# Attention and expert mixture on one core: corrected costs in a hand-written issue order, and a second home for late output tiles

## The chip, the cores and the metric

One of the eight cores of a Trainium2 chip runs the whole kernel. The core has a matmul engine (TensorE, PE in the profile, with its weight loads as PEld), VectorE (DVE), ScalarE (ACT), GpSimd (POOL) and SyncE (SP), each with an instruction queue of its own that it works off in order. The metric is the device time of one execution in microseconds (us); lower is better.

## The reference

Sliding-window attention with four sink tokens, then a mixture of four experts that every token passes through, weighted by its normalised domain probabilities. B, H, S, D are 4, 8, 768, 64; the mixture has N = 3072 tokens, width 512, inner width 1024.

```python
scores = q @ k.T / sqrt(D)
keep = (key < 4) | ((query - key >= 0) & (query - key < 128))
a = softmax(where(keep, scores, -1e9))
x = (a @ v) as [B * S, H * D]
p = domain_probs / (domain_probs.sum(-1) + 1e-9)
out = sum over e of  p[:, e] * (relu(x @ w1[e]) @ w2[e])
```

## The kernel before

Everything is computed in bf16 with float32 sums in PSUM. Tokens are worked on in groups of 256 (a pair of 128-token blocks): three groups g for each of four batches b. Attention for batch b goes by head pairs: scores (L676), exponentials on ScalarE (L701), a mask on VectorE (L695, L710), values (L735 for the sinks, L742 for the window), a reciprocal of the row sums (L769) and a scaling by it. For batch 0 the scaling is one VectorE instruction (L772) and the result is turned by PE (L800). For the other batches the scaling is four ScalarE instructions of 64 columns for each head pair (L781), and once all four head pairs of a group are scaled, one transposing DMA on SP's queue turns the group into `xT` (L759). The rows of q and k of these batches are turned by transposing DMAs too (L241).

The mixture's first layer comes in two forms. A slow unit (b, g, e) is four steps of eight matmuls of 256 columns (L1050) with a relu on ScalarE or VectorE. A fast unit is a Strassen-like form with seven products P1 to P7 of sixteen matmuls of 128 columns each (L1137). Its results are passed on through ScalarE copies (L1183, L1196) and VectorE additions (L1190, L1205), and gated results (L1170) go into the tile `H`. It needs sums and differences of the turned tokens (`T`, L1106) and of the weights. The second layer of batch 0 is plain: eight matmuls of 512 columns (L1382) for each 128 tokens and expert, gathered by VectorE (L1394). The second layer of batches 1 to 3 is again a seven-product form over pairs (b, g): P1, P2, P6, P5, P7, P3, P4, each of four pieces, one for each expert (L1311), with differences of `H` made on VectorE ("chores", L1234 and L1255). Two PSUM banks `acc` alternate. The results are copied or added into one output tile `osb` (L1354, L1339, L1342, L1347) and stored from it on SP's queue (L1344, L1303).

There is no scheduler at run time. The order of all instructions is written out by a planner in Python while the kernel is built. It keeps a clock `t` for each engine and prices what it has ordered: `pe`, `act`, `dve`, `pool`, `lands` for the loads on POOL's queue, `sp` for those on SP's. Work that follows a matmul waits in a list `pend` with a ready time and a slack, and `flush` gives it to ScalarE or VectorE by its due time. The loop at L1440 looks at each step that could come next on PE (a step of attention, of the first layer, a product piece, a second-layer step of batch 0), takes one that is planned to be ready within 40 ns, and among these the one of the lowest priority number:

```python
opts.append((max(p, now), HIGH_PRODUCT if behind > BEHIND or mix.live >= FULL else LOW_PRODUCT, "product", None))
opts += [(max(f, now), p, "first", x) for f, p, x in mix.firsts()]
```

A first-layer step of the open unit number i (0 or 1) has the priority 2 + `STEP0` x i, a new unit beside an open one `OPEN` = 2.6. A step of attention has 1.5 when it is due. If nothing is ready within 220 ns and the planned time is below 20 us, the planner orders one idle matmul (`idle_products`, L549) on a block of zeros.

The planned times matter only through the order: on the chip each instruction waits for its semaphores, and what stands behind it on its engine waits with it.

Of the kernel before, what the change touches and what calls it, by code (L numbers as in the profile page):

```python
# [11 lines left out]
FP32 = mybir.dt.float32  # L12
BF16 = mybir.dt.bfloat16
# [3 lines left out]
def kernel(  # L17
# [12 lines left out]
    nc = tc.nc  # L30

    B, H, S, D = q.shape
# [3 lines left out]
    Ntok, Dout = out.shape  # L36

    P = 128
# [13 lines left out]
    G = 2 * P  # L52
# [10 lines left out]
    SHARE_OF = (0.98, 0.90, 1.01)  # L63
    LEAD = (0.91, 0.90)
    DUE = 1.5
    LOW_PRODUCT = 2.015
    LOW_SECOND = 2.7
    HIGH_PRODUCT = 1.9
    EARLY = 0.01
    MASK = 2500  # L70
    GATE = 800
    GATE0 = 500
    FORM = 9000
    TOKEN = 1000
    MARGIN = 2000
    HOLD = 0
    FULL = 7
    STEP0 = 0.01
    READY = 40
    WIDE = 2  # L80
    OPEN = 2.6
# [1 line left out]
    ONE = 2  # L83
    PAIR = 1
    BEHIND = 1500
    CHORES = 6
    OWN = 2
    BIASED = 1
    FAST = tuple(START)
# [7 lines left out]
    t = {"pe": 1200.0, "act": 0.0, "dve": 0.0, "pool": 1280.0, "sp": 800.0, "sw": 6500.0, "hw": 0.0}  # L97
    ring, whole = [0.0] * 6, [False] * 6
    WARM = 6600.0
    FLIP, LATE = 300, 2500  # L100

    def pe(cols, *deps, n=1, switch=0):
        t["pe"] = max([t["pe"], *deps])
# [3 lines left out]

    def act(cols, *deps):
        at = max([t["act"], *deps])
        t["act"] = at + 75 + cols / 1.2  # L110
        return at + 205 + cols / 1.2

    def dve(cols, *deps, rate=0.96, fixed=157):
        at = max([t["dve"], *deps])
# [376 lines left out]
    load_v(0, (2, 3))  # L491
    load_w1(0, 2, [0])
    load_w1(0, 2, [1])
    t["sw"] += 700
    load_w2(0)

    nc.vector.tensor_copy(out=ident, in_=identf)
# [221 lines left out]
    def values(b, hp, g):  # L719

        ready = values_ready(b, hp, g)
        slot = pick()
        od = bank(slot, [P, 2, 2, DX], FP32, "od")
        a = aTs.pop((b, hp, g))
        cols = 0
        for qi in range(2):
            qb = 2 * g + qi
            terms = []
            c = 0
            for (kb, q0, nq) in GROUPS[g]:  # L730
                if q0 <= qb < q0 + nq:
                    terms.append((kb, c + (qb - q0) * P))
                c += nq * P
            if g > 0:
                nc.tensor.matmul(  # L735
                    od[:, qi], lhsT=sinkA[b][:, (qb - 2) * P:(qb - 1) * P], rhs=vsd[b][:, hp],
                    start=True, stop=False, skip_group_check=True,
                )
                cols += 2 * DX
            for ph in range(2):  # L740
                for i, (kb, c) in enumerate(terms):
                    nc.tensor.matmul(  # L742
                        od[:, qi, ph], lhsT=a[:, ph, c:c + P], rhs=vx[kb][:, 2 * hp + ph, 0:DX],
                        start=(g == 0 and i == 0), stop=(i == len(terms) - 1), skip_group_check=True,
                    )
                    cols += DX + 5
        done = pe(cols, ready)
        ring[slot] = 1e12
        if (b, g) not in onats:
            onats[b, g] = sb.tile([P, 2, NHP, P], BF16, name="onat", tag="onat", bufs=2)  # L750
        o = onats[b, g]

        def scaled(at):
            take(slot, at)
            onat_at[b, hp, g] = at
            onat_n[b, g] = onat_n.get((b, g), 0) + 1
            if b and onat_n[b, g] == NHP:
                xT[b, g] = sb.tile([P, 2, NHP, P], BF16, name="xT", tag="xT", bufs=2 * NG)
                nc.sync.dma_start(  # L759
                    out=xT[b, g].rearrange("c q h p -> c (q h) p"),  # L760
                    in_=o.rearrange("p q h c -> p (q h c)"), transpose=True,
                )
                turned_out = sp(at, issue=1330, takes=1400, turning=True)
                for x in range(NHP):
                    xT_at[b, x, g] = turned_out

        def run(engine):
            R = sb.tile([P, 2, 2, 1], FP32, name="R", tag="R", bufs=6)
            nc.vector.reciprocal(out=R, in_=od[:, :, :, D:DX])  # L769
            at = dve(4, fixed=171)  # L770
            if b < ONACT:
                nc.vector.tensor_mul(  # L772
                    o[:, :, hp].rearrange("p q (h d) -> p q h d", h=2), od[:, :, :, 0:D], R.to_broadcast([P, 2, 2, D]),
                )
                scaled(dve(2 * P))
                return

            def multiply(engine):
                for qi in range(2):
                    for ph in range(2):  # L780
                        nc.scalar.mul(o[:, qi, hp, ph * D:(ph + 1) * D], od[:, qi, ph, 0:D], R[:, qi, ph])  # L781
                        at = act(D)
                scaled(at)
            later("act", at, 600, multiply)
        later("dve", done, 500, run)
        values_at[b, g] = done
# [130 lines left out]
    class Mixture:  # L917


        def __init__(self):  # L920
            self.early = {g: list(range(E)) for g in range(NG)}
            self.open = []
            self.units = []
            for b, g in PAIRS:
                fast = [e for e in range(E) if self.is_fast(b, g, e)]
                slow = [e for e in range(E) if e not in fast]
                while fast or slow:
                    for x in (fast, slow):
                        if x:
                            self.units.append((b, g, x.pop(0)))  # L930
            self.order = list(self.units)
            self.T, self.T_at, self.fast, self.finished = {}, {}, {}, set()
            self.second, self.live, self.since, self.turn, self.credit = [], 0, 0, 0, 0.0
            self.H, self.H_at, self.H_part = {}, {}, {}
            self.S, self.S_at, self.waiting, self.last = {}, {}, [], []
            self.products = [(b, g, m) for b, g in PAIRS for m in CHAIN]
            self.piece, self.chores = 0, 0
            self.at, self.S4_at, self.C22 = {}, {}, {}
            self.done = 0.0
            self.stored = []  # L940
            self.spare, self.lent = [], {}

        def is_fast(self, b, g, e):
# [330 lines left out]
        def product_ready(self):  # L1274
            if not self.products:
                return 1e12
            b, g, m = self.products[0]
            e = self.order_of(b, g)[self.piece]
            at = (self.H_at if m in ("P1", "P2") else self.S4_at if m == "P3" else self.S_at).get((b, g, e), 1e12)
            bank = self.bank(b, g, m)  # L1280
            if self.piece == 0:
                at = max(at, acc_free[bank])
            if m == "P1" and self.piece == E - 1 and acc_free[1 - bank] > 1e11:
                at = 1e12
            if self.second or self.open and not self.open[0]["unit"][0] or any(self.early.values()):
                return 1e12
            return max(at, forms_at.get((e, m), 0.0 if m in ("P1", "P2", "P3") else 1e12))

# [6 lines left out]
        def emit_product(self):  # L1295
# [4 lines left out]
            r = (b * NQB + 2 * g) * P  # L1300

            def store(at, c=slice(0, Dout)):
                nc.sync.dma_start(out=out[r + P:r + 2 * P, c], in_=out_sb[b, g][:, 1, c])  # L1303
                sp(at)
            bank = self.bank(b, g, m)
            other = acc[1 - bank][:, 0:G]
# [16 lines left out]
                return  # L1323
            self.products.pop(0)
            if m == "P1":
                out_sb[b, g] = mo.tile([P, 2, Dout], FP32, name="osb", tag="osb", bufs=1)
                self.C22[b, g] = join(2, lambda at: store(at))
            o = out_sb[b, g]
            C11, C12, C21, C22 = o[:, 0, 0:G], o[:, 0, G:], o[:, 1, 0:G], o[:, 1, G:]
            acc_free[bank], seeded = 1e12, acc_free[1 - bank]  # L1330
            if m == "P1" and not final:
                acc_free[1 - bank] = 1e12
# [1 line left out]
            def run(engine):  # L1334
                if m == "P1" and not final:
                    nc.scalar.copy(out=other, in_=x)
                    acc_free[0] = acc_free[1] = act(G, seeded)
                elif m == "P2" and final:
                    nc.vector.tensor_add(C11, C11, x)  # L1339
                    acc_free[bank] = dve(G)  # L1340
                elif m == "P3":
                    nc.vector.tensor_add(C12, C12, x)  # L1342
                    acc_free[bank] = at = dve(G)
                    nc.sync.dma_start(out=out[r:r + P, :], in_=o[:, 0])  # L1344
                    sp(at)
                elif m == "P7":
                    nc.vector.tensor_add(C22, C22, x)  # L1347
                    acc_free[bank] = at = dve(G)
                    if final:
                        store(at, slice(G, Dout))  # L1350
                    else:
                        self.C22[b, g](at)
                else:
                    nc.scalar.copy(out={"P1": C11, "P2": C11, "P6": C12, "P5": C22, "P4": C21}[m], in_=x)  # L1354
                    acc_free[bank] = at = act(G)
                    if m == "P4" and final:
                        store(at, slice(0, G))
                    elif m == "P4":
                        self.C22[b, g](at)
# [189 lines left out]
```

## Time and profile before

| | |
|---|---|
| time, median of 3 runs | 368.44 us (367.04 to 370.63) |
| time of the profiled execution | 369.98 us |
| its span, first to last instruction | 368.1 us |
| mean granted clock of PE | 0.995 |
| PE busy | 356.0 us, 97% of the span |
| VectorE busy | 298.9 us, 81% |
| ScalarE busy | 162.5 us, 44% |
| POOL busy | 71.2 us, 19% |
| DMA | 37.25 MB in 117291 packets, 101 GB/s |

The page slices the span into 40 parts of 9.2 us and gives the busy share of each engine in tenths. A row of a timeline or of the waits names the engine, the line of the kernel, the tiles written and read, and in brackets how long the engine stood idle before and what ended the idle time. A wait of an engine costs time only if that engine's work, or what depends on it, sets the end.

### The profile page before, as it was taken

Reading aid. Unit: us, or ns where it says so; the run is one execution under the profiler, and the core shown is the slowest. Engines: PE = TensorE matmul, PEld = TensorE weight load, DVE = VectorE, ACT = ScalarE, POOL = GpSimd, SP = SyncE. Lnnn points to the kernel's source line nnn. Section 1 sums busy time; section 2 is a strip of 40 time slices with the busy share of each in tenths; the row PEclk is TensorE's granted clock in tenths of the full one; section 3 lists DMA queues with packets and bytes.
Section 4 is the critical chain, followed back from the end, with each engine's and each line's share of the span. In section 5 each row is a group of like instructions: output and inputs, shape, how many; then the busy total and the mean of one; then the engine's idle time right before and its main releaser. Section 6 shows DMA issues by size and latency. Waiting matters only on the chain.

```text
span 368.1 us, 10528 instructions
## 1 busy us (share of the span) xinstructions
PE 356.0 (97%) x4395; PEld 298.2 (81%) x4407; DVE 298.9 (81%) x671; ACT 162.5 (44%) x415; POOL 71.2 (19%) x92
## 2 busy tenths in 40 slices
PE   8789999999989999999999999999999999999996
PEld 4466666766668768898899899899999999999985
DVE  6743898976779869969879988979999898898930
ACT  5824643477636643555464545555113312213110
POOL 8926117403500805001430000000000000000000
PEclk9989999999999999999999999999999999999999
DMA  9999999999985999917999210212012011010011
GB/s 165 170 184 199 210 207 146 145 177 101 172 93 117 131 193 171 82 61 87 131 172 144 55 63 23 51 57 72 20 35 76 23 52 52 30 59 2 3 59 57
DMA packets 117291, 37.25 MB, mean 101 GB/s; under 512 B 100612, under 2 KB 112740, under 8 KB 117244
## 3 DMA queue, kind: packets, MB, share of 16 engines
q0 software_dynamic: 77520, 17.31, 53.0%
q1 hardware_dynamic: 38668, 18.75, 25.3%
q8 instruction: 34, 0.56, 0.6%
q10 hardware_dynamic: 1056, 0.52, 0.5%
q14 instruction: 13, 0.11, 0.1%
HBM read 40.45 MB, written 6.34 MB: 127 GB/s over the span
## 4 chain that ended last, share of the span: by engine, by line
PE 84%; DMA 6%; DVE 4%; ACT 3%; issue 1%; POOL 1%; ACTq 0%
PE cps L1137 29%; PE acc L1311 29%; PE hps L1050 11%; PE acc L1382 8%; DMA w<-in_moe_w_dram 2%; PE sps L676 2%; PE od L742 2%; ACT onat L781 2%; DMA xT<-onat 2%; DMA vx<-in_v_dram 1%; DMA out_dram<-osb 1%; PE od L735 1%; DVE H L1170 1%; PE tx L800 0%; ACT aT L701 0%
## 5 line engine op out<-in xcount | busy, mean ns | idle before, releaser
L1137 PEld LDWEIGHTS <-w 128*128 128x128 bf16 x1152 | 71.2, 98 | 3.8 <-issue 1.5
L1311 PEld LDWEIGHTS <-H 128*128 128x128 bf16 x600 | 55.9, 98 | 6.6 <-issue 0.9
L1050 PE MATMUL hps<-xT,w 128*128 128x256 bf16 x384 | 49.7, 278 | 3.7 <-DMA w<-in_moe_w_dram 2.8
L1170 DVE SCALAR_TENSOR_TENSOR H<-cps,gates 128x512 bf16<-128x512 f32 x78 | 52.5, 683 | 0.9
L701 ACT ACTIVATE aT<-sps 128x512 bf16<-128x512 f32 (+1 forms) x96 | 47.4, 582 | 13.1 <-PE sps L676 13.0
L1137 PEld LDWEIGHTS <-vf 128*128 128x128 bf16 x744 | 45.6, 98 | 2.1 <-issue 1.1
L1311 PE MATMUL acc<-w,H 128*128 128x256 bf16 x360 | 47.2, 273 | 0.0
L781 ACT ACTIVATE onat<-od,R 128x64 bf16<-128x64 f32 x144 | 33.0, 321 | 31.8 <-DVE R L769 26.5
L1050 PEld LDWEIGHTS <-w 128*128 128x128 bf16 x384 | 36.7, 100 | 10.5 <-DMA w<-in_moe_w_dram 3.0
L1382 PE MATMUL acc<-w,H 128*128 128x512 bf16 x180 | 43.8, 379 | 0.7 <-issue 0.2
L1137 PE MATMUL cps<-T,w 128*128 128x128 bf16 x576 | 43.9, 219 | 0.3 <-DVE cps L1190 0.3
L1137 PE MATMUL cps<-xT,w 128*128 128x128 bf16 x576 | 43.6, 219 | 0.2 <-ACT onat L781 0.2
L1183 ACT COPY cps<-cps 128x512 f32<-128x512 f32 x36 | 20.8, 576 | 44.8 <-PE cps L1137 43.3
L1354 ACT COPY osb<-acc 128x256 f32<-128x256 f32 x36 | 13.6, 378 | 57.6 <-PE acc L1311 54.1
L1137 PE MATMUL cps<-T,vf 128*128 128x128 bf16 x496 | 36.5, 219 | 0.1
L294 POOL DMA_DIRECT2D vx<-in_v_dram x24 | 21.6, 908 | 65.2 <-PE od L742 52.7
L1382 PEld LDWEIGHTS <-H 128*128 128x128 bf16 x192 | 18.0, 98 | 17.5 <-issue 0.2
L1311 PEld LDWEIGHTS <-S 128*128 128x128 bf16 x288 | 27.0, 98 | 4.3 <-issue 1.5
L1190 DVE TENSOR_TENSOR cps<-H,cps 128x512 f32<-128x512 f32 x30 | 20.7, 691 | 7.6 <-PE cps L1137 5.4
L1063 ACT ACTIVATE H<-hps 128x512 bf16<-128x512 f32 x26 | 15.5, 598 | 23.3 <-PE hps L1050 23.2
L1205 DVE TENSOR_TENSOR H<-H,cps 128x512 f32<-128x512 f32 x30 | 20.5, 683 | 5.3 <-PE cps L1137 5.2
L695 DVE TENSOR_TENSOR aT<-aT,mask 128x1024 bf16<-128x1024 bf16 (+1 forms) x36 | 22.7, 639 | 2.4 <-ACT aT L701 2.3
(125 smaller groups left out, 555.6 us busy)
## 6 DMA issues: line engine op xcount, KB each, us to landing
w<-in_moe_w_dram POOLq DMA_DIRECT2D x7, 1024.0 KB, 16.5
out_dram<-osb SPq DMA_DIRECT2D x23, 256.0 KB
gates<-gate_rows SPq DMA_DIRECT2D x36, 128.0 KB
vx<-in_v_dram POOLq DMA_DIRECT2D x24, 128.0 KB, 8.0
qkn<-in_q_dram POOLq DMA_DIRECT2D x22, 128.0 KB, 8.2
qkn<-in_k_dram POOLq DMA_DIRECT2D x22, 128.0 KB, 8.2
w<-in_moe_w_dram POOLq DMA_DIRECT2D x2, 512.0 KB, 9.6
kraw<-in_k_dram ACTq DMA_DIRECT2D x2, 256.0 KB
```

The source lines that it names most:

```text
L294: nc.gpsimd.dma_start(out=vx[tb][:, :, 0:D], in_=v[b, :, tb * P:(tb + 1) * P, :].rearrange("h p d -> p h d"),)
L695: nc.vector.tensor_mul(a, a, m[:, None, :].to_broadcast([P, 2, w]))
L701: nc.scalar.activation(out=a[:, ph], in_=sps[ph][:, 0:w], func=AF.Exp, scale=scale)
L781: nc.scalar.mul(o[:, qi, hp, ph * D:(ph + 1) * D], od[:, qi, ph, 0:D], R[:, qi, ph])
L1050: nc.tensor.matmul(h[:, i].rearrange("p (q n) -> p q n", q=2), lhsT=w1_sb[e][:, db, fb * P:(fb + 1) * P], rhs=xT[b, g][:, :, db], start=(i ...
L1137: nc.tensor.matmul(y[:, f], lhsT=A[:, d, f * P:(f + 1) * P], rhs=T[:, d], start=(m in ("P1", "P5") and f == 0 and d == 0), stop=(d == 1), ...
L1170: nc.vector.scalar_tensor_tensor(out=dst, in0=src, scalar=0.0, in1=gate, op0=ALU.max, op1=ALU.mult)
L1183: nc.scalar.copy(out=tiles["Y"], in_=y)
L1190: nc.vector.tensor_add(tiles["V"], c5, tiles["X"])
L1205: nc.vector.tensor_add(c5, c5, y)
L1311: nc.tensor.matmul(x, lhsT=self.operand(b, g, e, m)[:, f], rhs=forms[e][m][:, f], start=(k == 0 and f == 0 and m in (("P1", "P5", "P2") if ...
L1382: nc.tensor.matmul(op, lhsT=H[:, fb // QF, fb % QF, s], rhs=w2_sb[e][:, fb, :], start=(fb == 0), stop=(fb == NFB - 1),)
```

## The change

Prices and due times of the planner are set anew: `act` has a floor of 196 ns of engine time and 350 ns to its result; the two halves of the first expert's w1 are planned to land 1.4 and 0.6 us later, the loads behind them 0.6 us later; a group turned by the transposing DMA into `xT` is planned 1.5 us later (`SLOW`). Six constants change, among them the priorities of second-layer products (`LOW_PRODUCT`) and of the second open unit (`STEP0`), the slack of gated results (`GATE`) and the number of chores that may be pending at a time (`CHORES`). Products of the second layer are held back while any open unit belongs to batch 0, where before only the first open unit was asked. For pairs that begin after the last attention step, every other output tile is made of two `aT` buffers (bf16 tiles of attention, read as float32) in place of the one `osb` buffer. No computation is added or left out.

```diff
-    LOW_PRODUCT = 2.015
+    LOW_PRODUCT = 2.005
-    GATE = 800
+    GATE = 1500
-    STEP0 = 0.01
+    STEP0 = 0.3
-    CHORES = 6
+    CHORES = 2
-    FLIP, LATE = 300, 2500
+    FLIP, LATE, SLOW = 300, 2500, 1500
     def act(cols, *deps):
         at = max([t["act"], *deps])
-        t["act"] = at + 75 + cols / 1.2
-        return at + 205 + cols / 1.2
+        t["act"] = at + max(196, 68 + cols / 1.23)
+        return at + max(350, 205 + cols / 1.2)
...
     load_w1(0, 2, [1])
-    t["sw"] += 700
+    t["sw"] += 1300
+    landed["w1", 0, 0] += 1400
+    landed["w1", 0, 1] += 600
+    landed["w1", 0] += 600
     load_w2(0)
...
-                turned_out = sp(at, issue=1330, takes=1400, turning=True)
+                turned_out = sp(at, issue=1330, takes=1400, turning=True) + SLOW
...
-            if self.second or self.open and not self.open[0]["unit"][0] or any(self.early.values()):
+            if self.second or any(u["unit"][0] == 0 for u in self.open) or any(self.early.values()):
                 return 1e12
...
             if m == "P1":
-                out_sb[b, g] = mo.tile([P, 2, Dout], FP32, name="osb", tag="osb", bufs=1)
+                late = not att.more() and ahead == B - 1
+                if late and self.homed:
+                    x2 = [sb.tile([P, 2, 4 * P], BF16, name="aT", tag="aT", bufs=4) for _ in range(2)]
+                    out_sb[b, g] = [i.rearrange("p h w -> p (h w)").bitcast(FP32) for i in x2]
+                else:
+                    x2 = mo.tile([P, 2, Dout], FP32, name="osb", tag="osb", bufs=1)
+                    out_sb[b, g] = [x2[:, i] for i in range(2)]
+                self.homed = late and not self.homed
```

The stores and copies that use the output tile address its two halves accordingly; nothing else of them changes.

More of the change, by code (lines that the diff above doesn't have):

```diff
@@ L939, in __init__ @@
             self.done = 0.0
-            self.stored = []
+            self.stored, self.homed = [], False
             self.spare, self.lent = [], {}
@@ L1302, in store @@
             def store(at, c=slice(0, Dout)):
-                nc.sync.dma_start(out=out[r + P:r + 2 * P, c], in_=out_sb[b, g][:, 1, c])
+                nc.sync.dma_start(out=out[r + P:r + 2 * P, c], in_=out_sb[b, g][1][:, c])
                 sp(at)
@@ L1325, in emit_product @@
             if m == "P1":
-                out_sb[b, g] = mo.tile([P, 2, Dout], FP32, name="osb", tag="osb", bufs=1)
+                late = not att.more() and ahead == B - 1
[6 more added lines that the diff above has]
+                self.homed = late and not self.homed
                 self.C22[b, g] = join(2, lambda at: store(at))
             o = out_sb[b, g]
-            C11, C12, C21, C22 = o[:, 0, 0:G], o[:, 0, G:], o[:, 1, 0:G], o[:, 1, G:]
+            C11, C12, C21, C22 = o[0][:, 0:G], o[0][:, G:], o[1][:, 0:G], o[1][:, G:]
             acc_free[bank], seeded = 1e12, acc_free[1 - bank]
@@ L1343, in run @@
                     acc_free[bank] = at = dve(G)
-                    nc.sync.dma_start(out=out[r:r + P, :], in_=o[:, 0])
+                    nc.sync.dma_start(out=out[r:r + P, :], in_=o[0])
                     sp(at)
```

## The prediction

> **What bounds the kernel now.** I read the page's busy table first, then its slices, then what the matmul engine (PE) waited for, then the stretches around the longest waits, and last the tail. The page:
>
> ```profile
> PE 356.0 (97%) x4395; PEld 298.2 (81%) x4407; DVE 298.9 (81%) x671; ACT 162.5 (44%) x415; POOL 71.2 (19%) x92
> PE   8789999999989999999999999999999999999996
> PEclk9989999999999999999999999999999999999999
> ```
>
> PE is busy 356.0 of 368.1 us, so at most 12.1 us of idle time can be won, plus what a slow clock costs: the third slice of the clock is an 8. The waits of PE, and two long stretches:
>
> ```profile
> PE hps L1050 <- DMA w<-in_moe_w_dram: 2.8, 1, 2.8
> PE hps L1050 <- DVE H L1170: 0.9, 1, 0.9
> PE acc L1311 <- ACT osb L1354: 0.8, 1, 0.8
> PE sps L676 <- ACT onat L781: 0.7, 2, 0.4
> PE cps L1137 <- DVE cps L1190: 0.3, 1, 0.3
> ...
> 120.00:220.00 100.00, 99.90 (x1252) 85.58 (x1252) 85.53 (x197) 52.65 (x150) 23.29 (x28) 1.00 0.99 117
> 220.00:350.00 130.00, 129.69 (x1819) 121.96 (x1818) 118.03 (x249) 42.02 (x102) 0.00 (x0) 1.00 0.14 40
> ```
>
> The columns of the last two are PE, weight loads, VectorE (DVE), ScalarE (ACT) and POOL. From 120 to 350 us PE idles 0.10 + 0.31 = 0.41 us: no order can win more there. Whatever is won lies before 120 us or in the tail, each beside one named wait. DVE is at 118.03 of 130, 91%, so an order that bunches its work has little room.
>
> **The first w1: waiting and clock.** Rows at the wait, and the stretches around it (clock after the POOL column):
>
> ```profile
> 19.64 3.44 PE L1050 MATMUL hps<-xT,w 128*128 128x256 bf16 x16 [2.78 <-DMA w<-in_moe_w_dram]
> 22.92 0.22 PE L735 MATMUL od<-vsd,sinkA 128*128 128x130 bf16 x1
> 23.98 1.04 PE L1050 MATMUL hps<-xT,w 128*128 128x256 bf16 x8
> ...
> 15.90:19.30 3.40, 0.76 (x8) 0.27 (x7) 2.23 (x7) 3.05 (x7) 3.40 (x5) 1.00 1.24 202
> 19.30:22.80 3.50, 3.16 (x15) 2.19 (x16) 1.23 (x3) 0.00 (x0) 1.42 (x3) 0.51 1.21 196
> ```
>
> By the source's `lands()`, the planner has the first half of w1 at 17.0 us; it came at 19.6. Its due time now moves by 1.4 us to 18.4, the second half's by 0.6. The landing itself does not move: POOL issues the same transfers. What changes is what PE does meanwhile.
>
> Clock: after a stretch in which PE worked 0.76 of 3.40 us, the granted clock is 0.51, and 16 products take 3.44 us where a later row of the chain has 1.75 us for 16 of the same line. That is 1.69 us. The new due time makes PE fill with idle products (each some 0.1 us, ordered while nothing else is ready) or real work. With work until about 19 us the same stretch is about three quarters busy, and I take the clock as kept: gain 1.69. Bounds 0 and 1.69.
>
> Work moved ahead: three steps of values (L735, L742) lie between 22.92 and 23.98, 1.06 us. Their last operand, the exponentials of the sink tokens (L645), ends at 17.96 (17.48 start, 0.48 long), and three head pairs have their masks by 18.15. They fit before 19.6, so 1.06 us of real work replaces waiting. Bounds: 0, and the whole 2.78.
>
> What is late next is the second half of w1. It was issued at 11.63, and the median of 9.6 us for the two halves with 8.71 for the first gives 2 x 9.6 - 8.71 = 10.5 for the second: 22.1. PE arrives at 19.6 + 2 x 0.87 = 21.4. The three turns of the moved steps (0.69 us for three, row at 24.86) and a fourth values step cover about half, leaving 0.3 us. Sum: 1.69 + 1.06 - 0.3 = **2.45 us**; bounds -0.7 (nothing moved, clock lost, the whole 0.7 new) and 4.47.
>
> [...]
>
> **Scalings on ScalarE.** Planned: 75 + 64/1.2 = 128 ns each, 513 for four. The trace has four in 0.93 us with a last one of 0.32, so (0.93 - 0.32)/3 = 0.20 us apiece; the new 196 ns agrees. An exponential of 512 columns goes from 502 to 484 ns, masks and copies hardly move. No instruction is added: the planner only knows when ACT is free, so that scores whose banks wait behind scalings are ordered later. It can win PE's waits on L781, 0.7 + 0.2 = 0.9 us; nothing it moves costs less than zero, but a step put in between can be late in turn. Taken: **0.6**, bounds -0.3 (one wait on DVE as in the list above) and 0.9.
>
> **Turned tokens.** The transpose of xT goes out at 99.08 and DVE's token differences wait for it at the head of its queue:
>
> ```profile
> 106.45 0.29 DVE L1106 TENSOR_TENSOR T<-xT 128x256 bf16<-128x256 bf16 x1 [2.09 <-DMA xT<-onat]
> 108.38 0.61 PE L1137 MATMUL cps<-T,w 128*128 128x128 bf16 x8 [0.33 <-DVE cps L1190]
> 110.78 1.03 PE L1050 MATMUL hps<-xT,w 128*128 128x256 bf16 x8 [0.91 <-DVE H L1170]
> ```
>
> Behind the waiting L1106 stand L1394, L1190 and L1170, for which PE waits 0.33 + 0.91 = 1.24 us. `SLOW` makes planned xT 1.5 us later, so DVE gets other work first: 1.5 / 2.09 of 1.24 is **0.9**. Bounds: -0.3 (the products that need xT are ordered later too, and one waits like the 0.33) and 1.24.
>
> **Two homes late.** The tail:
>
> ```profile
> 352.26 10.17 SPq L1303 DMA_DIRECT2D out_dram<-osb  x2
> 355.72 0.37 ACT L1354 COPY osb<-acc 128x256 f32<-128x256 f32 x1 [3.48 <-DMA out_dram<-osb]
> 356.14 1.47 PE L1311 MATMUL acc<-wf,S 128*128 128x256 bf16 x12 [0.82 <-ACT osb L1354]
> ```
>
> The last pair's first copy waits for the store of the pair before out of the only `osb`; the third product needs the bank that this copy empties, and PE waits 0.82 us for it. With two `aT` buffers as the other home that wait has no reason: all readers of `aT` end with the last attention product, whose scaling is at 252.74. The alternation gives the second and fourth late pair the other home. Nine pairs of 28 product pieces run to 365 us, the last four of them with their first copies after 253 us, so the last is the fourth; were a fifth late, the last would have the old home. Next in line are P2's addition (0.42 us, then free to run at once) and DVE's differences L1234, needed only 5 us later. The final stores on SP keep their order. Gain **0.8**; bounds 0 (the last pair falls on the old home) and 0.82.
>
> **Order of products.** With `STEP0` 0.3 and `LOW_PRODUCT` 2.005, a second-layer product goes before the second open unit's first-layer products; before, it went after (2.01 against 2.015). `GATE`, `CHORES` and the stricter test in `product_ready` change what DVE takes first. Instruction counts hold, so the gain is at most 0.41 us. Loss: if PE meets late DVE results, the nearest rows are 0.33 and 0.91 us a piece. Since a step is ordered only when its operands are planned ready, and durations of DVE rows (0.68, 0.42) are near its planned ones, I take 0; it is the rival below. The cover is that 9% of DVE.
>
> **Sum.** 2.45 + 0.6 + 0.9 + 0.8 = 4.75. Span 368.1 - 4.75 = 363.35; the profiled execution is 369.98, of which 1.88 lie around the span, so it becomes 365.2. The median, 368.44, is 1.54 below that execution: **363.7 us**. All best bounds, 4.47 + 0.9 + 1.24 + 0.82 + 0.41 = 7.84, give 360.6; the worst of the named ones, 0.7 + 0.3 + 0.3 = 1.3 us, give 369.7 without the order.
>
> **Rivals.** *The early gain comes back.* PE now runs 2.5 us earlier into loads that keep their times; the slices of DMA show 9 tenths until about 90 us. Against it: the next expert's w1, issued at 22.43 with a median of 16.5 us to landing, is there at 38.9 or sooner, and its first use is at 41.7, 2.8 us of room. That is just enough. If it is not, the early 2.45 goes and 0.6 + 0.9 + 0.8 = 2.3 stays: 366.1 us. If instead only the clock still drops, 1.69 is lost: 365.4.
>
> *The new order starves the chains (slower).* Inside one fast unit, P7 and P3 wait for L1190, then P4 for L1205, each 0.69 us of DVE; today the other unit's products fill PE meanwhile. If products run ahead of the second unit, they are used up and PE has only the one chain: 0.91 us a time. For it: DVE's 91%. Against it: the second unit stays eligible whenever no product is ready. It decides when more than 4.75 / 0.91, about 5 units are hit; 10 of the some 20 units after 220 us would cost 9.1 us: 368.44 - 4.75 + 9.1 = 372.8 us.
>
> *The change does less than it says*: due times are still 1.2 us short (18.4 against 19.6), nothing is moved, and only the tail improves: 367.6 us.
>
> **Chances.** Forecast and anything better 0.58; gain partly returned or clock lost 0.24; only the tail 0.07; starved chains 0.11. A measurement of this kernel can tell about 1%, 3.7 us, from no change; the line is at 364.8, 1.1 us above the forecast. So faster takes the forecast's 0.58 less 0.03 near the line; same takes 0.03 + 0.24 + 0.07; slower takes half-serious and serious starvation, 0.11. The range leaves out the serious starvation and ends between its mild form and the worst bounds: 360.3 to 369.7.
>
> **What would show it.** Right: idle products up to about 18 us and none after; PE clock 1.00 from 19 to 23 us; L735/L742 ahead of the first L1050; no PE wait on `w` over 1 us; no DVE wait of 2 us for xT near 100 us; no ACT wait on `out_dram` in the tail. Wrong: PE under 99% between 120 and 350 us, new PE waits on DVE lines 1190, 1205 or 1255, or a later PE wait on `w` or `qkT`.

## The result and the profile after

The kernel after takes 364.75 us (median of 5 runs, 363.93 to 365.11); the kernel before, run beside it, 369.68 us (367.04 to 371.36). The ratio is 0.9869 with a 95% interval of 0.982 to 0.9918. So the gain beside it is 4.9 us by the medians. Against the 368.44 us that the prediction started from it is 3.7 us; that figure is a median of three runs, and 76 other runs of the kernel before, made beside the experiments, have a mean of 369.28 us. The profiled execution takes 364.39 us, its span 362.7 us, 5.4 us less than the span of before.

The page of the kernel after, its busy line and its PE slices:

```profile
PE 354.3 (98%) x4400; PEld 298.7 (82%) x4412; DVE 298.7 (82%) x669; ACT 164.1 (45%) x417; POOL 71.5 (20%) x92
...
PE   8899999899999999999999999999999999999996
```

PE is busy 1.7 us less, about what the slow clock had cost, and idle 8.4 us instead of 12.1. DVE and ACT do the same work as before. The waits of PE (sum, times, longest):

```profile
PE acc L552 <- DVE lent L463: 1.4, 1, 1.4
PE sps L679 <- DMA qkT<-qkn: 0.9, 1, 0.9
PE cps L1140 <- DVE cps L1193: 0.5, 1, 0.5
PE acc L1392 <- issue: 0.5, 3, 0.2
PE sps L679 <- DVE xT L265: 0.4, 1, 0.4
PE tx L803 <- DVE onat L775: 0.3, 2, 0.2
```

Lines have moved by 3 (by 10 behind the new output tile): L679 is L676 of before, L1053 is L1050, L1140 is L1137, L1314 is L1311, L1364 is L1354, L1392 is L1382. The waits for w1, for `osb`, for the scalings and for L1170 are gone. A wait for qkT, 0.91 us long, is new, and so is one of 0.53 us for L1193 (L1190 of before) at 123.8 us; the prediction had named both lines among its signs of being wrong. Three places of the timeline after (start, length, what, idle time before):

```profile
17.75 0.23 PE L738 MATMUL od<-vsd,sinkA 128*128 128x130 bf16 x1
...
18.48 0.49 PE L552 MATMUL acc<-lent 128*128 128x256 bf16 x3
...
18.91 1.05 PE L1053 MATMUL hps<-xT,w 128*128 128x256 bf16 x8
...
71.89 0.34 PE L679 MATMUL sps<-qkT 64*128 64x256 bf16 x4 [0.91 <-DMA qkT<-qkn]
...
349.12 0.37 ACT L1364 COPY osb<-acc 128x256 f32<-128x256 f32 x1 [1.38 <-PE acc L1314]
...
350.67 1.47 PE L1314 MATMUL acc<-wf,S 128*128 128x256 bf16 x12
```

Values and idle products stand ahead of the first w1 step, and no wait is noted there. In the tail ScalarE's first copy of the last pair waits for PE alone, and P6 starts without a wait. The stretches (PE, weight loads, DVE, ACT, POOL, then the granted clock):

```profile
15.90:19.30 3.40, 3.33 (x51) 2.12 (x50) 3.19 (x12) 3.40 (x9) 3.40 (x5) 1.00 1.23 197
19.30:22.80 3.50, 3.43 (x48) 2.86 (x46) 2.95 (x11) 1.81 (x4) 1.79 (x3) 1.00 1.20 189
...
120.00:220.00 100.00, 99.32 (x1317) 88.01 (x1316) 88.10 (x198) 52.85 (x151) 15.96 (x19) 1.00 0.88 105
220.00:350.00 130.00, 129.98 (x1792) 121.92 (x1790) 116.00 (x244) 40.51 (x98) 0.00 (x0) 1.00 0.16 42
```

The clock is 1.00 through. From 120 to 350 us PE idles 0.70 us instead of 0.41, the 0.53 us among it: nothing was won there.

**Where the time was won.** To compare kernels of different orders I count the columns that PE has streamed (each weight load times the columns of its matmuls, idle products left out) and note when the same count is reached. The table gives that time minus that of before, in us; 60 thousand columns are reached at 39.2 us in before, 140 at 74.0, 260 at 127.3, 500 at 229.5, 780 at 350.7, 800 at 360.2. A difference at the left also holds by how much w1 came earlier or later in that one execution, and that is much of it: the first half of w1 landed at 19.60 us in the profile of before, the second latest of the fourteen profiles, at 18.86 in after, 18.69 in slow_only and 18.38 in no_due. Slow_only and no_due have the old due times, waited for less long than before, kept the clock and stand at -2.39 and -2.75 all the same; order_only, whose w1 landed at 17.79 us, stands at some -3.3 by the same count. So the first column is not the worth of the due times.

```
columns, thousands     60     140     260     500     780     800
after               -3.05   -2.11   -4.37   -4.24   -4.26   -5.25
idle_only           -1.70   -1.69   -1.09   -0.31   -0.32   -1.30
due_only            -2.96   -2.37   +0.21   +1.12   +1.11   +0.13
homes_only          -0.01   -0.02   +0.23   +0.32   +0.31   -0.68
act_only            -1.00   -0.98   -1.99   -2.32   -2.65   -2.39
slow_only           -2.39   -0.71   -2.48   -1.78   -1.80   -1.77
due_slow            -2.97   -1.93   -3.13   -2.32   -2.34   -3.33
no_act_slow         -2.97   -1.28   -0.46   +0.43   +0.23   -0.75
no_due              -2.75   -2.72   -5.01   -5.14   -5.35   -6.33
late4               -3.40   -3.47   -6.43   -5.10   -5.31   -6.29
```

The kernel after wins 3.05 us by the first w1, gives 0.9 back by 74 us, wins 2.3 between 74 and 127 us, keeps that to 350 us, and wins 1.0 in the tail. Of the 3.05, 0.74 is that w1 landed earlier.

### The profile page after: what moved, and what is told of

It reads as the page before. It is cut to its first block, busy times and chain, and to the rows that moved or that the text cites. A ratio compares the mean times of both kernels' runs of the same rounds, so it can differ in the third digit from the quotient of the medians.

```text
span 362.7 us, 10537 instructions
## 1 busy us (share of the span) xinstructions
PE 354.3 (98%) x4400; PEld 298.7 (82%) x4412; DVE 298.7 (82%) x669; ACT 164.1 (45%) x417; POOL 71.5 (20%) x92
## 4 chain that ended last, share of the span: by engine, by line
PE 78%; DMA 16%; POOL 2%; DVE 1%; ACT 1%; issue 1%; SPq 0%
PE acc L1314 31%; PE cps L1140 29%; PE hps L1053 7%; DMA w<-in_moe_w_dram 7%; DMA qkn<-in_k_dram 6%; PE acc L1392 5%; DMA qkT<-qkn 3%; PE sps L679 2%; PE od L745 2%; POOL qkn L229 1%; PE od L738 1%; POOL vx L294 1%; ACT aT L704 1%; POOL sel L482 0%; PE sinks L640 0%
## 5 line engine op out<-in xcount | busy, mean ns | idle before, releaser
L1140 PEld LDWEIGHTS <-w 128*128 128x128 bf16 x1152 | 71.8, 98 | 4.4 <-issue 1.5
L1314 PEld LDWEIGHTS <-H 128*128 128x128 bf16 x600 | 55.8, 98 | 6.1 <-issue 0.6
L1140 PEld LDWEIGHTS <-vf 128*128 128x128 bf16 x744 | 45.9, 98 | 2.3 <-issue 0.8
L1314 PE MATMUL acc<-w,H 128*128 128x256 bf16 x360 | 47.7, 273 | 0.0
L1053 PE MATMUL hps<-xT,w 128*128 128x256 bf16 x384 | 47.3, 273 | 0.0
L1392 PE MATMUL acc<-w,H 128*128 128x512 bf16 x180 | 43.6, 379 | 0.9 <-issue 0.5
L1140 PE MATMUL cps<-T,w 128*128 128x128 bf16 x576 | 43.9, 219 | 0.5 <-DVE cps L1193 0.5
L1140 PE MATMUL cps<-xT,w 128*128 128x128 bf16 x576 | 43.4, 219 | 0.0
L1053 PEld LDWEIGHTS <-w 128*128 128x128 bf16 x384 | 36.1, 98 | 5.9 <-issue 0.8
L1140 PE MATMUL cps<-T,vf 128*128 128x128 bf16 x496 | 37.5, 219 | 0.0
L1392 PEld LDWEIGHTS <-H 128*128 128x128 bf16 x192 | 18.0, 98 | 18.1 <-issue 0.3
L1314 PEld LDWEIGHTS <-S 128*128 128x128 bf16 x288 | 27.0, 98 | 3.1 <-issue 0.4
L1193 DVE TENSOR_TENSOR cps<-H,cps 128x512 f32<-128x512 f32 x30 | 20.7, 691 | 9.3 <-PE cps L1140 9.3
L698 DVE TENSOR_TENSOR aT<-aT,mask 128x1024 bf16<-128x1024 bf16 (+1 forms) x36 | 22.8, 639 | 5.7 <-ACT aT L704 5.7
L1364 ACT COPY osb<-acc 128x256 f32<-128x256 f32 x28 | 10.5, 383 | 35.6 <-PE acc L1314 35.6
```

Source lines behind the costliest of these rows:

```text
L698: nc.vector.tensor_mul(a, a, m[:, None, :].to_broadcast([P, 2, w]))
L1053: nc.tensor.matmul(h[:, i].rearrange("p (q n) -> p q n", q=2), lhsT=w1_sb[e][:, db, fb * P:(fb + 1) * P], rhs=xT[b, g][:, :, db], start=(i ...
L1140: nc.tensor.matmul(y[:, f], lhsT=A[:, d, f * P:(f + 1) * P], rhs=T[:, d], start=(m in ("P1", "P5") and f == 0 and d == 0), stop=(d == 1), ...
L1193: nc.vector.tensor_add(tiles["V"], c5, tiles["X"])
L1314: nc.tensor.matmul(x, lhsT=self.operand(b, g, e, m)[:, f], rhs=forms[e][m][:, f], start=(k == 0 and f == 0 and m in (("P1", "P5", "P2") if ...
L1392: nc.tensor.matmul(op, lhsT=H[:, fb // QF, fb % QF, s], rhs=w2_sb[e][:, fb, :], start=(fb == 0), stop=(fb == NFB - 1),)
```

## The experiments

Ratios are to runs of the kernel before on the same chip, with their 95% intervals. The experiments ran on three chips, whose medians of the kernel before are 368.68, 369.32 and 369.79 us, so between experiments the ratio is the better guide. Where an edit adds lines, those behind it have moved: by 3 behind the new due times (L1053 in due_only is L1050) and behind the fill of idle_only, by 7 behind the new output tile alone (L1361 in homes_only is L1354).

**Idle products alone** (idle_only).

```diff
                 e = self.early[g].pop(0)
+                if not self.done:
+                    for _ in range(24):
+                        nc.tensor.matmul(acc[1][:, 0:G], lhsT=zeros[:, 0:P], rhs=zeros[:, 0:G], start=True, stop=True)
```

> The kernel before with 24 idle products of 256 columns put on PE just ahead of the first step of the first layer, and nothing else: the planner is not told of them, so the order of all other work is that of before. The theory of the prediction (PE's idleness before w1 halves the clock behind it): PE clock 1.00 from 19 to 23 us, the 16 products at the first w1 in about 1.75 us instead of 3.44, span shorter by about 1.7 us; w1 is waited for as before. [...] Second rival (what is won early is waited for again at loads): clock 1.00, but PE waits on w or qkT appear and the span is shorter by less than 0.8 us.

Measured: 368.38 us against 368.68, ratio 0.9983 (0.9956 to 1.0009). The clock stayed at 1.00, and the milestones are 1.7 us ahead until 74 us, as the theory had it; all twelve runs have a mean clock of 0.999 or 1.000, where 18 of the 35 of before on that chip are lower. But by 229 us 1.4 us of the lead is gone, as the second rival had it, though without a new wait on w or qkT: one on L1193 near 107 us is 0.93 us, where before has 0.33 on the same line. The timeline shows a cost of the fill as well:

```profile
16.81 2.78 PE L1021 MATMUL acc<-lent 128*128 128x256 bf16 x24
19.43 0.82 PE L1053 MATMUL hps<-xT,w 128*128 128x256 bf16 x6
```

w1 had landed at 18.05 us here, so the fixed fill held PE up by 1.4 us. What the clock gives, a fill of fixed length can take again.

**Due times alone** (due_only).

```diff
     load_w1(0, 2, [1])
-    t["sw"] += 700
+    t["sw"] += 1300
+    landed["w1", 0, 0] += 1400
+    landed["w1", 0, 1] += 600
+    landed["w1", 0] += 600
```

> The kernel before with only the due times of the first expert's w1 and of the loads behind it corrected. The theory: clock kept (1.69) and three values steps moved ahead of w1 (1.06), less some 0.3 of waiting for the second half of w1: span shorter by about 2.45 us, 0.75 more than with idle products alone. Rival (the early gain comes back at the loads): shorter by 1.7 us or less, with new PE waits on w or qkT before 90 us.

This kernel leaves out the stricter test, and its product pieces start at 132.4 us while second-layer steps of batch 0 run to 142.5 us in the same banks. So the sums of the two mix and its output is wrong; the amount of work is that of before, and what is read below lies ahead of 132 us. Measured: 368.20 us, ratio 0.9983 (0.9951 to 1.0014). The early 2.96 us are there; 0.6 is lost by 74 us, with a wait of 0.5 us for qkT, and the rest near 105 us. The rival had the loss right and most of its place wrong. The profile is of one of the three runs in twelve that lost a clock stretch (mean 370.35 us; the nine others 367.77). The timeline and two stretches:

```profile
103.80 0.29 DVE L1109 TENSOR_TENSOR T<-xT 128x256 bf16<-128x256 bf16 x1 [5.61 <-DMA xT<-onat]
...
105.48 1.03 PE L1053 MATMUL hps<-xT,w 128*128 128x256 bf16 x8 [1.67 <-DVE H L1068]
...
107.34 3.50 PE L1385 MATMUL acc<-w,H 128*128 128x512 bf16 x8 [0.83 <-DVE osb L1397]
```

```profile
104.00:107.40 3.40, 1.09 (x9) 0.83 (x9) 3.37 (x9) 1.74 (x4) 0.00 (x0) 1.00 0.44 48
107.40:110.80 3.40, 3.40 (x10) 1.27 (x10) 3.37 (x6) 0.00 (x0) 0.00 (x0) 0.51 0.74 174
```

VectorE stands 5.61 us at a token difference whose xT has not come; L1068 and L1397 stand behind it, PE waits for both, and the granted clock, 1.00 from 15.9 to 22.8 us, is 0.51 from 107.4 to 110.8 us: the eight products of L1385 take 3.50 us, where before has 1.73 for eight of the same line (L1382 there), some 1.7 more. Together that is 1.67 + 0.83 + 1.7 = 4.2 us. Without the clock it is 2.5 us, which no_act_slow below pays too.

**Two homes alone** (homes_only): the last hunk of the diff with its addressing.

```diff
+                late = not att.more() and ahead == B - 1
+                if late and self.homed:
+                    x2 = [sb.tile([P, 2, 4 * P], BF16, name="aT", tag="aT", bufs=4) for _ in range(2)]
...
```

> The kernel before with only the output tile in two homes late. The theory: the order is unchanged, the wait of ScalarE on out_dram before the last pair's first copy (3.48 us) and PE's 0.82 us behind it are gone, span shorter by 0.8 us. Rival (the tail then waits for the next thing, DVE's differences or the addition of P2): the wait is gone and PE waits elsewhere after 350 us, span shorter by less than 0.3 us.

Measured: 367.63 us against 368.68, ratio 0.9952 (0.9921 to 0.9983). The milestones move by 1.0 us between 780 and 800 thousand columns and nowhere else. The tail:

```profile
353.92 0.37 ACT L1361 COPY osb<-acc 128x256 f32<-128x256 f32 x1 [1.38 <-PE acc L1311]
...
355.46 1.47 PE L1311 MATMUL acc<-wf,S 128*128 128x256 bf16 x12
```

The theory holds; the gain is a little over its bound of 0.82.

**Constants of the order alone** (order_only).

```diff
-    LOW_PRODUCT = 2.015
+    LOW_PRODUCT = 2.005
...
-    GATE = 800
+    GATE = 1500
...
-    STEP0 = 0.01
+    STEP0 = 0.3
...
-    CHORES = 6
+    CHORES = 2
...
-            if self.second or self.open and not self.open[0]["unit"][0] or any(self.early.values()):
+            if self.second or any(u["unit"][0] == 0 for u in self.open) or any(self.early.values()):
```

> The kernel before with only the constants of the order (LOW_PRODUCT, STEP0, GATE, CHORES) and the stricter test before products. The theory: no gain and no loss, span within 0.5 us of before, PE above 99.5% busy from 120 to 350 us. Rival one (products ahead of the second open unit starve the chains): span longer by 2 us or more, PE waits on L1190 or L1205 in several units. Rival two (the new order, not the due times, is what made the kernel faster): span shorter by 1.5 us or more.

Measured: 369.81 us, ratio 1.0012 (0.9977 to 1.0047). Neither rival: no gain, no starved chain. The interval leaves a loss of up to 1.7 us open.

**Later tokens alone** (slow_only).

```diff
-                turned_out = sp(at, issue=1330, takes=1400, turning=True)
+                turned_out = sp(at, issue=1330, takes=1400, turning=True) + 1500
```

> The kernel before with only the turned tokens planned 1.5 us later (SLOW). The theory (VectorE's queue standing behind its token differences, which wait for xT, is what delays PE near 110 us): DVE's wait of 2.09 us at L1106 and PE's waits of 0.33 and 0.91 us are gone or under 0.5 us in sum, span shorter by about 0.9 us, the first w1 and the tail as before. Rival (the tokens are not the cause, the products that need xT are only put off): the waits move, span within 0.4 us of before.

Measured: 367.37 us against 369.32, ratio 0.9938 (0.9911 to 0.9965). It gains, between 140 and 260 thousand columns (from -0.71 to -2.48):

```profile
DVE T L1106 <- DMA xT<-onat: 3.8, 1, 3.8
```

The wait of 2.09 us at 106 us is gone, and so are PE's 0.33 and 0.91 us behind it. But VectorE waits 3.8 us for xT at 129 us, where before has 2.21; no wait of PE is noted behind either. So a wait on xT costs by what stands behind it.

**ScalarE prices alone** (act_only).

```diff
-        t["act"] = at + 75 + cols / 1.2
-        return at + 205 + cols / 1.2
+        t["act"] = at + max(196, 68 + cols / 1.23)
+        return at + max(350, 205 + cols / 1.2)
```

> The kernel before with only the new ScalarE prices. The theory: PE's waits for the scalings (0.7 and 0.2 us) are gone, span shorter by about 0.6 us. Rival (the order is disturbed for nothing): the waits for scalings shrink, but waits on L1190, qkT or xT of the same sum take their place, span within 0.4 us of before or longer.

Measured: 366.67 us against 369.32, ratio 0.993 (0.9906 to 0.9954): the largest effect of any part by the median, though its interval overlaps that of slow_only, and more than expected. PE's waits for the scalings are gone. The token stall is not: VectorE still waits for xT at 104 us, and PE for L1170:

```profile
104.46 0.29 DVE L1106 TENSOR_TENSOR T<-xT 128x256 bf16<-128x256 bf16 x1 [1.89 <-DMA xT<-onat]
108.78 1.03 PE L1050 MATMUL hps<-xT,w 128*128 128x256 bf16 x8 [0.90 <-DVE H L1170]
```

The granted clock was 0.51 here too, after a stretch in which PE had worked 1.85 of 3.40 us, more than half of the time:

```profile
15.20:18.60 3.40, 1.85 (x20) 0.80 (x18) 2.71 (x9) 3.40 (x9) 3.40 (x5) 1.00 1.23 203
18.60:22.00 3.40, 3.09 (x29) 2.61 (x30) 1.13 (x4) 0.83 (x2) 2.19 (x4) 0.51 1.18 192
```

**Due times, later tokens and the stricter test** (due_slow): the edits of due_only and slow_only together with the last two lines of order_only.

> The kernel before with the due times of the first w1, the later turned tokens and the stricter test before products; ScalarE prices, constants of the order and the one output tile as before. Due times alone lost all of an early 3.0 us again near 105 us, where VectorE stood 5.61 us for xT and the clock halved once more. The theory now: with xT planned later the early gain is kept, the milestones stay 2.5 us or more ahead of before up to 350 us, and the median falls by 2.5 to 3.5 us. Rival (PE ahead of the loads meets another transfer, qkT or q and k of the next batch, whatever is planned for xT): the early gain is down to 1 us or less by 140 us.

Measured: 366.29 us against 369.32, ratio 0.9919 (0.9885 to 0.9954): 3.0 us, inside what the theory expected. The milestones stay 2.3 us ahead, a little less than expected, where due times alone had lost everything.

**The kernel after without SLOW** (no_slow): `SLOW` 0.

> The kernel after with the turned tokens planned as before (SLOW 0). The theory: the early gain is kept to about 95 us and 1.5 us or more of it is lost near 105 us with a long DVE wait on xT; median 366 us or more, 1.2 us or more above the kernel after. Rival (prices of ScalarE and constants have already moved the tokens, so SLOW changes nothing): within 0.5 us of the kernel after, no DVE wait on xT over 2 us.

Measured: 364.19 us, ratio 0.9862 (0.9828 to 0.9896). My theory fell, the rival held: no wait of VectorE for xT is noted at all, and by the count of columns it is some 2.9 us ahead at 60 thousand and 4.3 at 260. In the kernel after SLOW is worth nothing.

**The kernel after without SLOW and without the ScalarE prices** (no_act_slow).

> The kernel after with both the ScalarE prices and the time of the turned tokens as before; due times, constants of the order, the stricter test and the two homes as after. Taking SLOW alone out of the kernel after cost nothing. Theory (ScalarE prices and SLOW each put the steps near 100 to 115 us in an order that keeps the early gain, so either is enough and both missing is what hurts): the early 3 us shrink by 2 us or more between 95 and 120 us, DVE waits on xT over 2 us, median 366.5 us or more. Rival (the constants of the order keep the gain, neither price does): within 0.7 us of the kernel after.

Measured: 367.58 us against 369.79, ratio 0.9931 (0.9901 to 0.9961), 2.8 us above the kernel after by the medians, 2.3 by the ratios. The early 2.97 us are down to 0.46 at 127 us. Of that, 1.7 are lost by 74 us, with a wait of 1.63 us for qkT. From 74 to 127 us this kernel loses 0.8 against before, where due_slow wins 1.2 and the kernel after 2.3; VectorE's row is that of due_only again:

```profile
104.82 0.29 DVE L1109 TENSOR_TENSOR T<-xT 128x256 bf16<-128x256 bf16 x1 [5.56 <-DMA xT<-onat]
```

PE's waits behind it are 1.62 and 0.83 us, 2.45 in sum, and the clock held at 1.00 from 104.0 to 110.8 us. With no_slow and due_slow this shows that either correction keeps what due_only loses near 105 us and that both missing loses it: the stricter test and the constants stand in no_act_slow too and do not keep it. How much is lost at qkT by 74 us differs from kernel to kernel (0.5 to 1.6 us of waiting, none in some), and why was not tried beyond late4.

**The kernel after with the old due times** (no_due): the edit of due_only undone.

> The kernel after with the due times of the first w1 and of the loads behind it as before. Theory: PE idles before w1 again, for 0.8 to 2.8 us by how late the transfer is in that execution, and in some executions the clock halves behind it; part of what is lost comes back because PE no longer waits 0.9 us on qkT at 71 us; median 1 to 2.5 us above the kernel after, its runs spread over 3 us or more. Rival (the early gain is all given back later): within 0.5 us of the kernel after, no wider spread.

Measured: 365.18 us (363.55 to 365.50), ratio 0.987 (0.9831 to 0.9909), 0.4 us above the kernel after by the median and the same by the ratio; the theory expected 1 to 2.5. Three of the six runs have the lower mean clock, as it expected, and the spread is 2 us. In its profile PE waits for w1, and the granted clock is 1.00 from 15.9 to 22.8 us:

```profile
18.43 1.05 PE L1050 MATMUL hps<-xT,w 128*128 128x256 bf16 x8 [1.50 <-DMA w<-in_moe_w_dram]
```

There is no wait on qkT later, and the milestones are ahead of those of the kernel after by 140 thousand columns: what the kernel after has more at 39 us (0.3) is given back there. In this execution w1 landed 0.48 us earlier than in that of the kernel after, so the two profiles alone do not price the due times; the runs do.

**The kernel after with the old constants** (no_order): the first eight lines of order_only undone, the stricter test kept.

> The kernel after with LOW_PRODUCT, STEP0, GATE and CHORES as before; the stricter test stays. Theory: the constants are worth nothing either way, within 0.7 us of the kernel after. Rival (they gain beside corrected prices, though not alone): 1 us or more above the kernel after, with PE waits on L1193, L1208 or L1173 between 120 and 350 us.

Measured: 364.22 us, ratio 0.987 (0.9831 to 0.991), that of the kernel after. No worth of the constants is seen, either way.

**A try at a faster one** (late4).

```diff
-    FLIP, LATE, SLOW = 300, 2500, 1500
+    FLIP, LATE, SLOW = 300, 4000, 1500
```

> The kernel after with the rows turned for scores planned 1.5 us later still (LATE 4000 in place of 2500), a try at a faster version. Theory: PE's wait of 0.91 us on qkT at 71 us is gone, other work stands there, and the median is 0.5 to 0.9 us below the kernel after. Rival (the wait is on the loads' pace, PE has nothing else that is worth doing first, or later steps are put off too): within 0.4 us of the kernel after, or above it.

Measured: 363.59 us (363.51 to 364.44), ratio 0.9843 (0.9808 to 0.9879). The wait on qkT is gone; other products stand in its place:

```profile
71.36 1.89 PE L1392 MATMUL acc<-w,H 128*128 128x512 bf16 x7
73.19 0.34 PE L679 MATMUL sps<-qkT 64*128 64x256 bf16 x4
```

The median is 1.2 us under that of the kernel after. The intervals of the two ratios overlap, so a faster kernel is likely, not shown.

## Why the prediction was right, and where its steps were not

Forecast 363.7 us, measured 364.75, inside the range and on the forecast side. Most of the miss of 1.05 us is the starting point: 368.44 us was 0.84 below the mean of the other 76 runs. The gain forecast was 4.75 us; from mean to mean it is 369.28 - 364.59 = 4.69. That it came so close is luck: as the list shows, the terms for w1 and tokens were too large by some 2.2 us together, ScalarE and the tail too small by 1.1, and 1.0 us belongs to no single term. One measurement helps to size them: in the trace of before the clock is at half for 3.41 us behind the wait for w1 (19.37 to 22.78 us), and in due_only and act_only it is 0.51 over 3.40 us. A stretch of 3.4 us at half clock lowers the mean granted clock of an execution by 0.5 x 3.4 / 368 = 0.0046. From that I estimate how many each run had: none at a listed clock of about 1.000, one at 0.995, two at 0.991.

```
                  runs   none            one             two
before              76   30: 368.11 us   35: 369.71 us   11: 371.06 us
after                5    5: 364.59 us
no_due               6    3: 364.22 us    3: 365.22 us
```

The figures are counts and mean times; those of before are over all its runs beside the experiments.

- **The clock** (priced 1.69). Cause right: with the new due times 49 of 54 runs in all kernels have no such stretch (a mean clock of 0.998 or more), with the old ones, idle_only aside, 55 of 130. The size is about right for an execution of before that has one, which is 1.60 us longer (369.71 - 368.11). That is not the price of a stretch everywhere: the runs with one are longer by 1.0 us in slow_only and in no_due, and by 0.2 in act_only (366.77 - 366.57, eight runs against four). But not each execution has it. On average before lost 369.28 - 368.11 = 1.17 us. The profiled execution had one and was 1.54 us above the median of that time; I took 1.69 off the median in full. That step is over-sized by some 0.5 us.
- **Work moved ahead** (1.06, less 0.3). Two values steps were moved, not three, 17.75 to 18.48, so 0.73; the wait for the second half of w1 did not come. But 0.91 is paid again at qkT: the first rival, in part. Taken out of the kernel after (no_due), the due times are worth 0.4 us in the median, nothing in the ratio, and nothing at equal clock: 364.22 against 364.59, on three and five runs that spread over 2 and 1.2 us. What they do is keep the clock: three of the six runs of no_due have one stretch at half clock, none of the five of the kernel after.
- **ScalarE** (0.6, bound 0.9). Under-sized. Alone at equal clock it gives 368.11 - 366.57 = 1.5 us, more than the two waits that I had bounded it by. I priced the waits that carry the name of the scalings; the order between 74 and 127 us also changed. Which step of the new order wins the rest is not shown.
- **Tokens** (0.9). The mechanism is right, and due_only and no_act_slow show it larger than in before. The size depends on company: 368.11 - 366.79 = 1.3 us alone at equal clock, nothing in the kernel after (no_slow). Adding it to the sum as a term of its own was the fault. The ScalarE prices alone do not cure the same stall (0.90 us on L1170 is left in act_only); in no_slow it is gone, and which edits beside them that needs was not tried.
- **Tail** (0.8). Right in kind, a little small: 1.0 us by the milestones. The parity was not as I had it: five pairs are late, so the last one has `osb` again and the pair before it `aT`. That costs nothing, since what matters is that two neighbours differ; the bound of 0 for this term had no ground.
- **Order** (0). No gain and no loss is seen; the slower rival did not occur. The constants are four, and `SLOW` is the fifth, not six as said ahead of the prediction.

With equal clock the kernel after is 368.11 - 364.59 = 3.5 us faster. ScalarE prices alone (1.5) and the tail (1.0) make 2.5 of it. The other 1.0 is not in any part taken out singly: no_slow, no_due and no_order are all at 364.2 to 364.4 at equal clock. Which of the corrections together give it stays open.

On the clock the profiles show this much. PE worked 0.76 us (before, 15.90 to 19.30), 1.09 (due_only, 104.00 to 107.40) and 1.85 (act_only, 15.20 to 18.60) of 3.40 us, and the granted clock of the stretch behind was 0.51 each time. It worked 1.63 us (no_act_slow, 104.00 to 107.40) and 1.90 (no_due, 15.90 to 19.30) of 3.40, and the clock behind was 1.00. Behind waits for w1 of 2.8 (before), 2.4 (homes_only) and 1.8 us (act_only) the granted clock was 0.51, 0.73 (both 19.30 to 22.80) and 0.51 (18.60 to 22.00); with waits of 1.5 (no_due), 0.8 (order_only) and 0.8 us (no_order) it was 1.00 from 15.90 to 22.80. Since 1.85 us of work was followed by the low clock and 1.63 was not, the work in such a stretch does not decide alone; what does is not shown.

## What to carry to other kernels

A corrected time is worth what the next late thing allows: an early lead of 3 us was lost to a transfer at 72 us and to one in-order VectorE queue that stood 5.6 us behind another, and the second loss, 2.5 us of PE waiting, all but went once either of two other prices was right. So correct and test prices together. A price taken from one profiled execution must be weighed with how often other executions show the same thing; the mean clock of each run tells that without a profile. The same holds for two profiles set side by side: before was taken when its w1 came late. A part that gains alone can be worth nothing beside the others (SLOW, 1.3 us and nothing), so take parts out of the whole as well as putting them in alone.

## What was not expected of the hardware

The same w1 transfer, issued at 10.9 us by the same instruction, let its first step begin at 17.83 (order_only), 18.43 (no_due) and 19.64 us (before) where PE waited for it, so one due time cannot be right for all. In act_only PE was more than half busy over 3.40 us (1.85), and the granted clock was still 0.51 over the next 3.40. In due_only, with waits of 1.67 and 0.83 us in the middle of dense work, it was 0.51 over 3.40 us too, though no_act_slow, with waits of 1.62 and 0.83 us at that place, kept 1.00. Between 104.00 and 107.40 us PE worked 1.09 us in due_only and 1.63 in no_act_slow; whether that is what tells the two apart is not shown.
